# Other slots for the gate terms, the loads, the fold and the finishing of an mLSTM and Fourier-mix kernel

## The chip, the cores and the metric

The kernel runs on one core of a Trainium2 chip. Its time is the device time of one execution in microseconds (us). Several runs were taken, and the median of them stands for the kernel. One further execution was recorded by the hardware profiler. The engines are called PE or TensorE (matrix products; PEld is its weight load), DVE or VectorE, ACT or ScalarE, POOL or GpSimd, and SP or SyncE, which issues the DMAs here. Every engine works through its own instructions in the order of the program.

## The reference

Two blocks follow each other. The first is an mLSTM cell over batch 4, 8 heads, 768 steps and head size 40; the second is a Fourier mix with an MLP over rows of 8 * 40 = 320 features.

```python
for t in range(S):
    m_new = np.maximum(f_gate[:, :, t] + m, i_gate[:, :, t])
    f_stab, i_stab = np.exp(f_gate[:, :, t] + m - m_new), np.exp(i_gate[:, :, t] - m_new)
    C = f_stab[..., None, None] * C + i_stab[..., None, None] * np.einsum('bhd,bhe->bhde', vt, kt)
    n = f_stab[..., None] * n + i_stab[..., None] * kt
    h_tilde = np.einsum('bhde,bhe->bhd', C, qt)
    y[:, :, t] = sigmoid(o_gate[:, :, t]) * h_tilde / np.maximum(np.abs(n . qt), 1.0)
x = y as (B, S, 320)
u = x + real(fft(fft(x, axis=1), axis=2))
un = (u - mean(u)) / sqrt(var(u) + 1e-06)
out = u + np.maximum(un @ w_ch1, 0.0) @ w_ch2        # 320 -> 1280 -> 320
```

## The kernel before

All arithmetic is fp32. The recurrence is done in six chunks of 128 steps for each batch. A chunk needs the stabilising maximum, the decay and the weights of its steps; these gate terms are computed for all 32 (batch, head) rows at once in `gates`. Batch 0 works with whole chunks (`plan_mlstm`), batches 1 to 3 with half chunks (`plan_halves`), for which `gates_of_halves` makes other gate terms in nine numbered steps: step 0 the maxima at the half boundaries (GpSimd, with one VectorE instruction `nexts`, L327), step 1 the rows `keep` in the order of the chunks (ScalarE copies L335 to L341, GpSimd L342 and L343), step 2 one exponential of `between` (L345), twelve exponentials for the decays (L349), and all stores of `keep` and of the decays to the DRAM tensors `M_d` (12 DMAs, L357) and `G_d` (L359), step 3 twelve exponentials for the weights (L364), step 4 a GpSimd product (L368), steps 5 to 8 transposes and copies. The chunks of batches 1 to 3 read `M_d` and `G_d` back, spread over partitions, as `W` (L496) and `Gb` (L505).

A chunk of half-chunk kind goes through: loads (`mlstm_load`, `mlstm_load_max`, `mlstm_load_decay`), `qg` on GpSimd (`mlstm_scale_q`, L528), `vw` on GpSimd (`mlstm_scale_v`, L534), eight exponentials on ScalarE (`mlstm_exp`, L518), two masks on GpSimd (L543), scores and state sums on TensorE (`halves_scores`, `halves_to_state`, one PSUM tile of two banks), decay of the state on GpSimd (L696), add and weigh on VectorE (L703, L708), products with the state and the chunk on TensorE (`halves_from_state`, `halves_from_chunk`, a second PSUM tile), and `mlstm_finish` on VectorE (L752 to L759), which writes the rows of x.

The Fourier mix folds pairs of chunks (`mix_fold`, three pairs, VectorE and GpSimd), multiplies the folds with a table along the sequence (`mix_seq`, `mix_tail`, PSUM tiles `pz` and `pzt`), then along the features (`mix_feat`, `pu`), adds to x (`mix_add`), centres on ScalarE (`mix_center`), transposes on TensorE (`mix_turn`, `put`) and copies to `uT`. Before the change, batches 2 and 3 fold a second time (`mix_fold_again`, two VectorE instructions) and use the products of `mix_products_again`; batches 0 and 1 use `mix_products`. The MLP of batch 0 is plain (`mlp_in` L1067 and L1058, `mlp_relu`, `mlp_out` L1192); the MLPs of batches 1 to 3 go by blocks with fewer products (`mlp_block` L1129, `mlp_out_pair` L1248, `residual` L1198, `hidden_sums` L1234).

The weights come as float64 bits in ten pieces. Each is loaded, and rebuilt in fp32 by `take` (VectorE L436, L438), `convert` (ScalarE L443, L444) and `join` (VectorE L450, L452, L456).

The order of the work is written out by hand. `at(slot, phase, fn, ...)` puts a step into a slot and a phase in it, and `run` emits all in sorted order:

```python
def run(end=None):
    for key in sorted(plan):
        if end is None or key[0] < end:
            for fn, args in plan.pop(key):
                fn(*args)

EVAC, FILL, MAIN, FILL_PE = range(4)
```

So EVAC comes first in a slot, then FILL, MAIN and FILL_PE. Batch 0's mLSTM fills slots 0 to 21, its mix slots 18 to 28, its MLP slots 31 to 62 (`mlp_in` 31 to 50, `mlp_out` 51 to 62); the MLP of batch b begins at slot 31 + 32 b. Batch 1's mLSTM begins at slot 32 and its mix at 54; batch 2's at 51 and 83; batch 3's at 83 and 115. The step of chunk c counts from s = start + 3 c: scores at s, add and weigh at s + 1, from_state at s + 3, finish at s + 4. Two sets of memory change hands between two calls of `run`: the pool of the gates and four PSUM banks of batch 0 are closed, and the buffers of the later MLPs and the two PSUM tiles of the half chunks are opened; before, this is after slot 27.

PSUM tiles named by `bank` take one of four banks, either from a list written by hand (`turn`) or by a number. `idle_products` are products of zeros.

Of the kernel before, what the change touches and what calls it, by code (L numbers as in the profile page):

```python
# [19 lines left out]
L = 128  # L20
NT = S // L
NP = H // 2
# [35 lines left out]
def kernel(  # L58
# [83 lines left out]
    def idle_products(n, first=False):  # L142
        pw = bank("pi", [L, 2 * L]) if first else ps_s.tile([L, 2 * L], FP, name="pi", tag="ps")
        for i in range(n):
            nc.tensor.matmul(pw, rest[:, 0:L], rest, start=True, stop=True, skip_group_check=True)


    def gates(gp):
# [168 lines left out]
        def gates_of_halves(step):  # L317
# [15 lines left out]
            elif step == 1:  # L333
# [8 lines left out]
                nc.gpsimd.tensor_copy(out=W[:, 0:4:3, L - 1:L], in_=late["nexts"][:, 1:5:3])  # L342
                nc.gpsimd.tensor_copy(out=W[:, 4, LH:LH + 1], in_=late["nexts"][:, 5])  # L343
            elif step == 2:
                nc.scalar.activation(out=late["between"], in_=late["between"], func=AF.Exp)  # L345
                for c in range(NT):
                    for i in range(2):
                        t = slice(i * LH, (i + 1) * LH)
                        nc.scalar.activation(out=G[:, c, t], in_=W[:, c, t], func=AF.Exp, scale=-1.0,  # L349
                                             bias=late["starts"][:, c, i:i + 1])  # L350
                nc.sync.dma_start(out=sp_sb, in_=first_heads)
                for b in range(1, B):
                    for hip in range(2):
                        rows = slice(b * H + hip * NP, b * H + (hip + 1) * NP)
                        for i in range(2):
                            slot = slice(b * H + i * NP, b * H + (i + 1) * NP)
                            nc.sync.dma_start(out=M_d[:, i ^ hip, slot].rearrange("c p t -> p c t"),  # L357
                                              in_=W[rows, :, i * LH:(i + 1) * LH])
                nc.sync.dma_start(out=G_d[:, H:].rearrange("c p t -> p c t"), in_=G[H:BH])  # L359
            elif step == 3:  # L360
# [10 lines left out]
            elif step in (5, 7):  # L371
# [10 lines left out]
                if step == 5:  # L382
                    nc.tensor.matmul(late["pd"], spread_sb[:, 0:L], late["dec2"], start=True, stop=True)
            else:
                j = (step - 6) // 2
# [18 lines left out]
        at(7, FILL + 0.5, clear, fe[:, :, NC:PAD], fe[:, :, PAD + HALF_D - 1:], fe_odd[:, NC:])  # L404
        for n, (s, phase) in enumerate(((15, FILL + 0.75), (16, FILL + 0.75), (18, FILL + 0.75), (19, FILL + 0.75),
                                        (18, FILL + 0.8), (19, FILL_PE + 0.5), (20, FILL + 0.75),
                                        (21, FILL_PE + 0.5), (22, FILL + 0.75))):
            at(s, phase, gates_of_halves, n)
# [373 lines left out]
    def plan_halves(b, s0, stride=3):  # L782
        at(s0 - 2, FILL + 0.7, halves_start, b)
        for c in range(NT):
            s = s0 + stride * c
            end = c == NT - 1
            t = 22 + 2 * c if b == 1 and c < 3 else s - 6
            at(t, FILL, mlstm_load, b, c)
            at(t, FILL, mlstm_load_max, b, c)
            at(t + 1 if c < 2 or b > 1 else s - 5, FILL, mlstm_load_decay, b, c)  # L790
            at(s - 2, FILL, mlstm_load_o, b, c)
            at(s - 2, FILL + 0.1, mlstm_scale_q, b, c)
            at(s - 2, FILL + 0.15, halves_alone, b, c)
# [70 lines left out]
    def mix_seq(b, p, parts):  # L864
# [3 lines left out]
        if p == TG - 1:  # L868
            k.pz = getattr(k, "pz", []) + [bank("pz", [L, NK], MIX["z"][i] if b > 1 else None) for i in parts]
        for i in parts:  # L870
            if b < 2:
                mix_products(p, k.pz[i], i, slice(0, L))
# [4 lines left out]
    def mix_tail(b, p):  # L877

        k = mixes[b]
        if p == TG - 1:  # L880
            k.pzt = bank("pzt", [L, NK], MIX["zt"] if b > 1 else None)
        halves = [k.pzt[i * 64:(i + 1) * 64] for i in range(2)]
        if b < 2:
            for i in range(2):
# [43 lines left out]
    def mix_feat(b, p):  # L928
# [5 lines left out]
        m = slice(COL[p], COL[p] + L)  # L934
        pu = k.pu[p] = bank("pu", [L, DM + 1 + NC], MIX["u"][p] if b > 1 else None)
        if b == 0:
# [47 lines left out]
    def mix_turn(b, c):  # L984

        k = mixes[b]
        pt = k.pt[c] = bank("put", [L, 3, L], MIX["ut"][ORDER.index(c)] if b > 1 else None)
        for ch in range(3):
# [335 lines left out]
    def plan_batch(b, s_mlstm, s_mix, s_mlp):  # L1324
# [192 lines left out]
```

## Time and profile before

| what | us |
|---|---|
| median of three runs | 407.24 |
| lowest and highest run | 404.89, 408.12 |
| the profiled execution, its own time | 404.67 |
| span of its profile | 402.9 |
| TensorE idle after 30 us, the sum of its gaps of more than 0.1 us | 10.0 |
| first L1067 (slot 31) | 59.53 |
| first L1192 (slot 51) | 117.68 |
| first L1129 (slot 63) | 171.22 |
| first L1248 (slot 83) | 209.77 |

The profile is read like this. A row of a timeline has start, length, engine, line and operation, output and inputs, shapes, count, and in brackets the idle time of the engine ahead of it with what ended it. A row of the waits has who waited for whom, the total, the number of times and the longest. An fp32 product shows as two records. A row of the windows has the window, its length, the busy time and count of PE, PEld, DVE, ACT and POOL, the granted TensorE clock as a share of full speed, the DMA share and GB/s. The mean granted clock of the execution is 0.991.

### The profile page before, as it was taken

How to read it: one execution, taken by the hardware profiler on the slowest of the kernel's cores; microseconds unless marked ns; L12 is line 12 of the kernel's file. 1: busy time of each engine (PE TensorE's matmuls, PEld its weight loads, DVE VectorE, ACT ScalarE, POOL GpSimd, SP SyncE). 2: the span in 40 equal slices, each digit the busy share in tenths (PEclk: the TensorE clock that was granted, in tenths of full speed). 3: DMA queues.
4: the chain of work that ended last, by engine and by line, in shares of the span. 5: the costliest groups of instructions: out<-in, count | busy, mean ns of one | idle time of the engine just before them, and what ended most of it. 6: DMA issues, size and time to landing. Idle time of an engine off the chain costs nothing.

```text
span 402.9 us, 10837 instructions
## 1 busy us (share of the span) xinstructions
PE 387.8 (96%) x4324; PEld 283.3 (70%) x4324; DVE 279.8 (69%) x668; ACT 178.5 (44%) x513; POOL 128.0 (32%) x231
## 2 busy tenths in 40 slices
PE   8999999999969999999999998999999999999996
PEld 6887555556546776856569887855579997556996
DVE  7789976898867519787665689777663795336652
ACT  6898867576530213553562214544440023454000
POOL 5744425466945412261145304351200000020000
PEclk9999999989989999999999999999999999999999
DMA  7979499677752424365100525300000000000000
GB/s 197 278 227 320 121 240 257 194 242 240 191 151 70 142 87 131 109 196 150 54 26 2 157 82 170 103 20 2 1 0 18 17 34 33 2 0 0 34 34 34
DMA packets 22766, 43.96 MB, mean 109 GB/s; under 512 B 3492, under 2 KB 11388, under 8 KB 22588
## 3 DMA queue, kind: packets, MB, share of 16 engines
q1 hardware_dynamic: 22716, 43.27, 36.0%
q8 instruction: 34, 0.56, 0.5%
q14 instruction: 16, 0.13, 0.1%
HBM read 39.16 MB, written 4.10 MB: 107 GB/s over the span
## 4 chain that ended last, share of the span: by engine, by line
PE 80%; DVE 13%; issue 2%; POOL 2%; ACT 2%; DMA 0%; DVEq 0%; SPq 0%; POOLq 0%; ACTq 0%
PE po L1248 20%; PE pm L1129 16%; PE po L1192 8%; PE pm L1134 6%; PE ph L547 5%; PE ps L547 4%; PE pu L946 4%; PE pm L1067 4%; PE put L989 2%; PE pz L903 1%; PE pz L915 1%; DVE so L756 1%; PE pM L230 1%; PE pm L1058 1%; DVE x L759 1%
## 5 line engine op out<-in xcount | busy, mean ns | idle before, releaser
L1138 DVE TENSOR_TENSOR h<-h,pm 128x384 f32<-128x384 f32 x60 | 30.7, 550 | 30.6 <-PE pm L1129 16.5
L1198 DVE SCALAR_TENSOR_TENSOR x<-po,rstd,x 128x160 f32<-128x160 f32 (+1 forms) x69 | 27.0, 394 | 35.0 <-PE po L1248 32.3
L1129 PE MATMUL pm<-uT,w_sb 128*128 128x384 f32 x90 | 37.8, 507 | 0.2 <-DVE uT L1117 0.2
L543 POOL TENSOR_SCALAR_AFFINE_SELECT W<-W 64x512 f32<-64x512 f32 x36 | 27.9, 775 | 31.5 <-ACT W L518 30.4
L696 POOL TENSOR_TENSOR C<-C,decB 128x164 f32<-128x164 f32 x33 | 17.4, 528 | 62.1 <-DVE C L703 58.4
L518 ACT ACTIVATE W<-W,colT 128x64 f32<-128x64 f32 x144 | 36.5, 338 | 0.0
L1192 PE MATMUL po<-w_sb,h 128*128 128x320 f32 x120 | 35.2, 444 | 0.0
L1013 POOL TENSOR_TENSOR t<-rstd 128x6 f32<-128x6 f32 x12 | 2.6, 216 | 90.1 <-DVE v L1007 89.7
L1248 PE MATMUL po<-T,S 128*128 128x160 f32 x180 | 28.1, 303 | 2.6 <-DVE x L1198 2.6
L528 POOL TENSOR_TENSOR qg<-qk,Gb 128x512 f32<-128x512 f32 x21 | 27.3, 1298 | 9.5 <-DMA Gb<-G_d 9.5
L1192 PEld LDWEIGHTS po<-w_sb,h 128*128 128x128 f32 x120 | 22.7, 194 | 10.0 <-issue 1.5
L1067 PE MATMUL pm<-uT,w_sb 128*128 128x384 f32 x80 | 29.5, 505 | 0.1
L1248 PEld LDWEIGHTS po<-T,S 128*128 128x128 f32 x180 | 25.3, 190 | 4.5 <-DVE x L1198 3.4
L1248 PE MATMUL po<-w_sb,h 128*128 128x160 f32 x180 | 26.3, 300 | 0.0
L1248 PEld LDWEIGHTS po<-w_sb,h 128*128 128x128 f32 x180 | 25.2, 190 | 1.5 <-DVE x L1198 0.3
L994 ACT COPY uT<-put 128x384 f32<-128x384 f32 x24 | 11.1, 478 | 32.7 <-PE put L989 32.6
L1134 PE MATMUL pm<-uT,w1t_sb 64*128 64x384 f32 x120 | 25.2, 510 | 0.2 <-DVE h L1138 0.2
L1129 PEld LDWEIGHTS pm<-uT,w_sb 128*128 128x128 f32 x90 | 15.4, 189 | 14.0 <-DVE h L1138 4.9
L1185 ACT ACTIVATE h<-h 128x384 f32<-128x384 f32 x45 | 23.1, 520 | 2.0 <-DVE h L1138 2.0
L982 ACT ACTIVATE uc<-x 128x384 f32<-128x384 f32 x24 | 14.5, 614 | 18.9 <-DVE x L974 18.9
L703 DVE TENSOR_TENSOR C<-C,ps 128x164 f32<-128x164 f32 x33 | 10.5, 317 | 16.2 <-PE ps L547 13.6
L1067 PEld LDWEIGHTS pm<-uT,w_sb 128*128 128x128 f32 x80 | 14.5, 194 | 9.7 <-issue 1.4
(240 smaller groups left out, 860.8 us busy)
## 6 DMA issues: line engine op xcount, KB each, us to landing
kvt<-in_kv SPq DMA_DIRECT2D x24, 336.0 KB
qk<-in_qkT SPq DMA_DIRECT2D x48, 160.0 KB
raw<-in_w SPq DMA_DIRECT2D x10, 640.0 KB
Gb<-G_d SPq DMA_DIRECT2D x42, 128.0 KB
W<-M_d SPq DMA_DIRECT2D x36, 128.0 KB
so<-in_o SPq DMA_DIRECT2D x24, 160.0 KB
out<-x SPq DMA_DIRECT2D x24, 160.0 KB
ds_sb<-in_dft_s SPq DMA_DIRECT2D x1, 1158.0 KB
```

Of the source, the lines that this page charges most:

```text
L518: nc.scalar.activation(out=k.W[:, h, :], in_=M, func=AF.Exp, scale=-1.0, bias=colT[:, c, 0, b * H + h:b * H + h + 1])
L528: nc.gpsimd.tensor_tensor(out=k.qg[:, :, t], in0=k.qk[:, 0, :, t], in1=k.Gb[:, :, t], op=OP.mult)
L543: nc.gpsimd.affine_select(out=W, in_=W, compare_op=OP.is_ge, fill=0.0, base=base, pattern=[[0, H], [-1 if back else 1, LH]], channel_multi ...
L547: nc.tensor.matmul(out, w, x, start=start, stop=True, skip_group_check=True)
L1067: nc.tensor.matmul(k.pm[i], w1_sb[:, ch, f0:f0 + L], u[2 * ch], start=(ch == 0 and not ahead), stop=(ch == 1 and ahead), skip_group_check= ...
L1129: nc.tensor.matmul(bank, w, u, start=start, stop=True, skip_group_check=True)
L1134: nc.tensor.matmul(bank, block(w1t_sb, i)[rows], mlp_u(gr, 1)[rows], start=False, stop=True, skip_group_check=True)
L1138: nc.vector.tensor_tensor(out=h, in0=h, in1=bank, op=OP.add)
L1185: nc.scalar.activation(out=h, in_=h, func=AF.Relu, scale=-1.0)
L1192: nc.tensor.matmul(k.po, hidden(gr, f)[:, i * L:(i + 1) * L], w2_sb[:, f, :], start=(f == 0), stop=(f == NFF - 1))
L1198: nc.vector.scalar_tensor_tensor(out=u, in0=po, scalar=k.rstd[:, c:c + 1], in1=u, op0=OP.mult, op1=OP.add)
L1248: nc.tensor.matmul(po, a[:, f], w[:, f], start=start and f == 0, stop=f == half - 1, skip_group_check=True)
```

## The change

The gate terms of the half chunks are made earlier: step 0 in slot 8 for 15, step 1 in slot 10 for 16 and with the exponential of `between`, step 4 in slot 11 for 18. The stores leave step 2 and become steps of their own: `M_d` in slot 13, `G_d` in slot 20; steps 2, 3 and 5 to 8 stay. Batch 1's mLSTM begins at slot 29 for 32 and its mix at 51 for 54; its first three chunks are loaded in slots 15, 18 and 21 for 22, 24 and 26, with the decays in 21, 22 and 27. Its first scores and state sums go to slot 25 (vw to 24), and the change of memory is after slot 24. Batch 1 uses the second fold and its products, and the banks by number; `mlp_out` of batch 0 alternates banks 0 and 1. The last five weight pieces move by one slot at most and are taken and converted in one slot. `mlstm_finish` of batches 2 and 3 moves from FILL to behind MAIN of its slot. One idle product of three goes.

```diff
     def idle_products(n, first=False):
-        pw = bank("pi", [L, 2 * L]) if first else ps_s.tile([L, 2 * L], FP, name="pi", tag="ps")
+        if first:
+            pw = bank("pi", [L, 2 * L])
+        elif "heads" in banks:
+            pw = banks["heads"][:, 0, 0:2 * L]
+        else:
+            pw = ps_s.tile([L, 2 * L], FP, name="pi", tag="ps")
...
+                nc.scalar.activation(out=late["between"], in_=late["between"], func=AF.Exp)
             elif step == 2:
-                nc.scalar.activation(out=late["between"], in_=late["between"], func=AF.Exp)
...
-                nc.sync.dma_start(out=sp_sb, in_=first_heads)
-                for b in range(1, B):
...
-                nc.sync.dma_start(out=G_d[:, H:].rearrange("c p t -> p c t"), in_=G[H:BH])
...
+            elif step == 9:
+                nc.sync.dma_start(out=sp_sb, in_=first_heads)
+                for b in range(1, B):
...
+            elif step == 10:
+                nc.sync.dma_start(out=G_d[:, H:].rearrange("c p t -> p c t"), in_=G[H:BH])
...
-        for n, (s, phase) in enumerate(((15, FILL + 0.75), (16, FILL + 0.75), (18, FILL + 0.75), (19, FILL + 0.75),
-                                        (18, FILL + 0.8), (19, FILL_PE + 0.5), (20, FILL + 0.75),
-                                        (21, FILL_PE + 0.5), (22, FILL + 0.75))):
+        for n, (s, phase) in enumerate(((8, FILL + 0.75), (10, FILL + 0.75), (18, FILL + 0.75), (19, FILL + 0.75),
+                                        (11, FILL + 0.8), (19, FILL_PE + 0.5), (20, FILL + 0.75),
+                                        (21, FILL_PE + 0.5), (22, FILL + 0.75), (13, FILL + 0.9), (20, FILL + 0.9))):
...
-            t = 22 + 2 * c if b == 1 and c < 3 else s - 6
-            at(t, FILL, mlstm_load, b, c)
-            at(t, FILL, mlstm_load_max, b, c)
-            at(t + 1 if c < 2 or b > 1 else s - 5, FILL, mlstm_load_decay, b, c)
+            t, g = ((15, 21), (18, 22), (21, 27))[c] if b == 1 and c < 3 else (s - 6, s - 5)
+            at(t, FILL + 0.9, mlstm_load, b, c)
+            at(t, FILL + 0.9, mlstm_load_max, b, c)
+            at(g, FILL + 0.9, mlstm_load_decay, b, c)
...
-            at(s - 1, FILL, mlstm_scale_v, b, c)
+            first = b == 1 and c == 0
+            at(24 if first else s - 1, FILL, mlstm_scale_v, b, c)
...
-            at(s, FILL_PE + 2.05, halves_scores, b, c)
-            at(s, FILL_PE + 2.5, halves_to_state, b, c)
+            at(25 if first else s, FILL_PE + (5.6 if first else 2.05), halves_scores, b, c)
+            at(25 if first else s, FILL_PE + (5.6 if first else 2.5), halves_to_state, b, c)
...
-            at(s + 4 + int((b, c) in ((2, 2), (3, 1))), FILL + 0.05, mlstm_finish, b, c)
+            late = int((b, c) in ((2, 2), (3, 1)))
+            at(s + 4 + late, (FILL + 0.05 if b == 1 else MAIN + 0.4), mlstm_finish, b, c)
...
-            if b < 2:
+            if b == 0:
                 mix_products(p, k.pz[i], i, slice(0, L))
...
-            elif b == 1 or j == 0:
-                if b > 1:
-                    for step, slot in enumerate((x_done[-1] + 2, x_done[-1] + 6)):
-                        at(slot, FILL_PE + 0.25, mix_fold_again, b, step)
+            elif j == 0:
+                for step in range(2):
+                    at(*((x_done[-1], FILL + 0.55) if b == 1 else (x_done[-1] + 2 + 4 * step, FILL_PE + 0.25)),
+                       mix_fold_again, b, step)
...
-            k.po = bank("po", [L, DM])
+            k.po = bank("po", [L, DM], (gr * TG + i) % 2)
...
-            feat = [s_mix + c for c in ((3, 4, 6) if b == 1 else (3, 4, 7))]
-            add = [s_mix + c for c in ((4, 4, 5, 6, 7, 7) if b == 1 else (4, 4, 5, 6, 8, 9))]
-            turn = [s_mix + c for c in ((5, 6, 6) if b == 1 else (6, 7, 8))]
-            late = [s_mix + c for c in ((7, 8, 8) if b == 1 else (9, 10, 10))]
+            feat = [s_mix + c for c in (3, 4, 7)]
+            add = [s_mix + c for c in (4, 4, 5, 6, 8, 9)]
+            turn = [s_mix + c for c in (6, 7, 8)]
+            late = [s_mix + c for c in (9, 10, 10)]
...
-    plan_batch(1, 32, 54, s_mlp + MLP_SLOTS)
+    plan_batch(1, 29, 51, s_mlp + MLP_SLOTS)
...
-    when += [((33, 0.7), (35, 0.7), (36, 0.6))] + [((s, 0.7), (s + 1, 0.7), (s + 2, 0.6)) for s in (36, 39, 42, 45)]
+    when += [((s, 0.6), (s, 0.7), (s + 1, 0.6)) for s in (34, 37, 40, 43, 46)]
...
-    for s, phase, n in ((24, 5.5, 1), (25, 5.5, 1), (26, 5.5, 1)):
+    for s, phase, n in ((24, 5.5, 1), (26, 5.5, 1)):
         at(s, FILL_PE + phase, idle_products, n)
-    run(28)
+    run(25)
```

Where `if b > 1 else None` chose a bank of the mix before, it now reads `if b > 0 else None`, for `pz`, `pzt`, `pu` and `put`.

More of the change, by code (lines that the diff above doesn't have):

```diff
@@ L350, in gates_of_halves @@
                                              bias=late["starts"][:, c, i:i + 1])
-                nc.sync.dma_start(out=sp_sb, in_=first_heads)
-                for b in range(1, B):
[L353 to L358, printed above, removed]
-                nc.sync.dma_start(out=G_d[:, H:].rearrange("c p t -> p c t"), in_=G[H:BH])
             elif step == 3:
@@ L383, in gates_of_halves @@
                     nc.tensor.matmul(late["pd"], spread_sb[:, 0:L], late["dec2"], start=True, stop=True)
+            elif step == 9:
+                nc.sync.dma_start(out=sp_sb, in_=first_heads)
+                for b in range(1, B):
+                    for hip in range(2):
+                        rows = slice(b * H + hip * NP, b * H + (hip + 1) * NP)
+                        for i in range(2):
+                            slot = slice(b * H + i * NP, b * H + (i + 1) * NP)
+                            nc.sync.dma_start(out=M_d[:, i ^ hip, slot].rearrange("c p t -> p c t"),
+                                              in_=W[rows, :, i * LH:(i + 1) * LH])
+            elif step == 10:
+                nc.sync.dma_start(out=G_d[:, H:].rearrange("c p t -> p c t"), in_=G[H:BH])
             else:
@@ L868, in mix_seq @@
         if p == TG - 1:
-            k.pz = getattr(k, "pz", []) + [bank("pz", [L, NK], MIX["z"][i] if b > 1 else None) for i in parts]
+            k.pz = getattr(k, "pz", []) + [bank("pz", [L, NK], MIX["z"][i] if b > 0 else None) for i in parts]
         for i in parts:
-            if b < 2:
+            if b == 0:
                 mix_products(p, k.pz[i], i, slice(0, L))
@@ L880, in mix_tail @@
         if p == TG - 1:
-            k.pzt = bank("pzt", [L, NK], MIX["zt"] if b > 1 else None)
+            k.pzt = bank("pzt", [L, NK], MIX["zt"] if b > 0 else None)
         halves = [k.pzt[i * 64:(i + 1) * 64] for i in range(2)]
-        if b < 2:
+        if b == 0:
             for i in range(2):
@@ L934, in mix_feat @@
         m = slice(COL[p], COL[p] + L)
-        pu = k.pu[p] = bank("pu", [L, DM + 1 + NC], MIX["u"][p] if b > 1 else None)
+        pu = k.pu[p] = bank("pu", [L, DM + 1 + NC], MIX["u"][p] if b > 0 else None)
         if b == 0:
@@ L986, in mix_turn @@
         k = mixes[b]
-        pt = k.pt[c] = bank("put", [L, 3, L], MIX["ut"][ORDER.index(c)] if b > 1 else None)
+        pt = k.pt[c] = bank("put", [L, 3, L], MIX["ut"][ORDER.index(c)] if b > 0 else None)
         for ch in range(3):
```

## The prediction

> **What bounds the kernel now.** I read the busy table first, then a table of stages, then TensorE's waits, and then, inside the stages that lose time, the engines' timelines.
>
> ```profile
> PE 387.8 (96%) x4324; PEld 283.3 (70%) x4324; DVE 279.8 (69%) x668; ACT 178.5 (44%) x513; POOL 128.0 (32%) x231
> ```
>
> TensorE (PE) is the bound over the span of 402.9 us, so only TensorE time saved, or a TensorE wait removed, can pay. The stage table (window, length, busy PE, PEld, DVE, ACT, POOL, clock, DMA share, GB/s) says where there is any:
>
> ```profile
> 32.00:40.00 8.00, 7.10 (x106) 5.76 (x103) 7.51 (x22) 6.57 (x20) 3.46 (x10) 1.00 1.03 342
> 40.00:48.00 8.00, 7.15 (x53) 4.77 (x53) 7.21 (x19) 6.28 (x25) 4.90 (x10) 1.00 0.30 100
> 60.00:118.00 58.00, 53.91 (x920) 33.28 (x919) 46.41 (x98) 36.16 (x109) 35.31 (x53) 0.95 0.76 218
> 118.00:174.00 56.00, 56.00 (x750) 39.79 (x752) 36.20 (x92) 16.50 (x54) 21.50 (x30) 0.99 0.34 109
> ```
>
> 60 to 118 is batch 0's first MLP product with batch 1's mLSTM filled in (slots 31 to 50): 4.1 us idle, and the clock is below 1. From 118 on TensorE never stops. The waits of TensorE name the releasers:
>
> ```profile
> PE ph L547 <- DVE x L759: 3.1, 1, 3.1
> PE po L1248 <- DVE x L1198: 2.6, 2, 1.9
> PE ps L547 <- DVE C L703: 1.0, 1, 1.0
> PE ph L581 <- POOL qg L528: 0.9, 1, 0.9
> ```
>
> All the large ones are VectorE (DVE) being late. Two finer windows carry the half clock that follows:
>
> ```profile
> 80.00:88.00 8.00, 7.00 (x134) 5.14 (x126) 7.76 (x16) 5.75 (x17) 4.45 (x7) 0.79 0.72 228
> ...
> 112.00:120.00 8.00, 5.94 (x76) 3.68 (x77) 5.20 (x16) 3.29 (x12) 4.51 (x12) 0.79 0.48 138
> ```
>
> 0.79 over 8 us is 3.4 us at half rate, so 1.7 us lost each time, after the 1.0 and the 3.1 us wait. VectorE's own rows before the second:
>
> ```profile
> 109.77 1.77 DVE L456 TENSOR_TENSOR w_sb<-m,e 128x640 f32<-128x640 f32 x1
> 111.47 0.31 DVE L703 TENSOR_TENSOR C<-C,ps 128x164 f32<-128x164 f32 x1
> ...
> 113.52 0.49 DVE L759 TENSOR_TENSOR x<-ph,so 128x320 f32<-128x320 f32 x1
> ```
>
> A weight pass (L456, alone 0.82 us) stands ahead of the mLSTM work and takes 1.77, because GpSimd (POOL) runs a 1.84 us qg from 109.01. This recurs all over the trace: a VectorE row with all inputs in SBUF (L456, L756, L836) that starts during a GpSimd row ends one own length after it.
>
> **The change part by part.** The profiled execution is 404.67 us (span 402.9 and 1.77 around it); the median shown is 407.24. I work out differences and put them on the median.
>
> *(1) Gate terms, slots 15/16/18 to 8/10/11.* In the trace they stand here on GpSimd:
>
> ```profile
> 34.37 0.20 POOL L326 TENSOR_TENSOR a<-a,F 32x5 f32<-32x5 f32 x1
> ...
> 34.69 0.26 POOL L331 TENSOR_SCALAR less<-M 32x6 f32<-32x6 f32 x1
> 37.67 0.22 POOL L331 TENSOR_SCALAR less<-nexts 32x5 f32<-32x5 f32 x1 [2.73 <-DVE nexts L327]
> ...
> 38.47 1.25 POOL L528 TENSOR_TENSOR qg<-qk,Gb 128x512 f32<-128x512 f32 x1
> ```
>
> The queue stood 2.7 us for one small VectorE row, and chunk 5's qg behind it cost TensorE 0.9. In slot 8 the same knot recurs: nexts now follows the weight join of slot 8 (L450 25.25 to L456's end), so GpSimd waits from 24.95 to about 27.8 and then runs less, less, between (0.7), vw (0.73) and chunk 3's qg (1.24): qg ends at 30.5, where TensorE wants it at 29.14 (L581). That is a new wait of 1.3. It passes down TensorE's queue; ScalarE gets 1.2 us of copies and the exponential (L335 to L345) ahead of chunk 4's eight exponentials, so chunk 5's weights come 1.2 later (39.15 for 37.94). VectorE is contiguous from 25.25 to 49.15 and sets the end. It wins L456's stall (1.0) and, with L368 (0.84) gone from slot 18, most of L836's at 44.44 (0.9); it loses about as much where L756, L436 and L438 meet the crowded GpSimd at 29 to 37, and then waits for the exponentials. I get +1.0. Bounds: -2.0 (only the wins) and +3.9 (the whole 2.9 wait and one 1.0 stall). The DMAs: 12 M_d stores took 4.5 us of SP's queue at 41.0; now they stand at 31 to 36, ahead of chunk 5's so load (36.03, read at 43.28) and batch 1's first loads: 2 us late with 5 us of cover, zero. The G_d store stays behind its exponentials at slot 20; Gb of batch 1 still lands 2 us or more before slot 27's qg: zero; without that cover it costs what is left of the 1.27 us qg.
>
> *(2) Chunk (1,0)'s scores and state sums in slot 25* (two TensorE groups, 1.07 us at 63.15), where an idle product stood. TensorE is waiting there for ScalarE's centred rows (put at 57.20 and 58.41): 57.6 + 1.07 = 58.67, so the last put is 0.26 late: +0.3 (0 to +1.07). vw in slot 24 (0.74) has its data at 51.2. The dropped idle product (0.4) was inside the wait: 0.
>
> *(3) Slots 31 to 51, batch 1 three slots earlier, weight passes after the mLSTM's add.* Before: 59.53 to 122.55, the end of batch 2's first scores, 63.0 us. TensorE's work in it after the change: 80 records of L1067 by 0.355 start to start 28.4; 40 of L1058 by 0.2125 8.5; three put 1.0; one pu 1.8; mLSTM groups 3 by 1.88 (71.93 to 73.81), 2 by 2.33 (105.80 to 108.13), the last 1.08: 11.4; first half of po 2.7; batch 2's scores 1.07. Sum 54.9. Check on before: 54.9 + 1.07 + 4.1 idle + 3.4 lost to clock = 63.5 against 63.0. Waits that I expect in their place: 1.2 in slot 32 (chunk (1,0)'s eight exponentials can start only after the last uT copy, 59.47; 2.0 of them, 1.6 of masks, decay, add, so the state is ready at 63.9 where TensorE asks at 63.1, and the scores 0.4 later); 1.0 in slot 47 (from_state of chunk 5 needs finish of chunk 4; VectorE's period there is add and weigh 1.1, finish 1.65, weight pass 3.3, fold 1.9, stalls 0.9, so 8.9 against TensorE's 7); 1.6 in slot 49 (the relu that frees its bank stands on ScalarE behind the last piece's conversion, which waits for that late VectorE). 54.9 + 3.8 = 58.7: -4.3. Bounds: -8.1 (no wait) and -0.6 (waits and clock as before, the sum's 0.5 error off).
>
> A gap's after-cost is the clock. Here 1.0 and 3.1 us of wait were each followed by 3.4 us at half rate, while 1.85 us at 248.0 was followed by none; I put none on the shorter waits, 1.7 each in the bound. The Trainium skill, TensorE: Matmul & The Clock Gate (HAM oscillation), says instead that gaps hurt from about 3.4 us; by it neither dip of this trace would exist, the part would be worth 3.4 less wherever I count recovered clock, and 401.3 below would read 404.7. The rows decide.
>
> *(4) Folding batch 1 twice.* Batch 1's pz and pzt now: 132.63 to 134.72, 137.41 to 139.35, 142.14 to 144.28, 6.17 us. The same three pieces of batch 2, which already folds twice: 1.47 + 1.33 + 1.52 = 4.32. TensorE is full there: -1.85 (0 if VectorE's two added passes, 0.55 + 0.68, come last; -1.85 else). New banks and the two po banks: TensorE has no gap in 118 to 174 and each bank has two slots to drain: 0, or 0.35 per residual if not.
>
> *(5) Finishing of batches 2 and 3 behind the slot's products.* In slot 91 VectorE runs finish (247.80 to 249.44) before the residual that TensorE waits for, the 1.85 row; swapped, the residual is ready at 248.2: -1.65. In slot 87 finish began during the product; it now starts after the second residual (231.4) and ends at 233.0 for 232.44, which delays the next residual: +0.55. The other ten lie where TensorE did not wait: 0. Sum -1.1 (-1.65 to +0.55).
>
> Total: 1.0 + 0.3 - 4.3 - 1.85 - 1.1 = -5.95. **401.3 us** on the median (398.7 for the profiled run).
>
> **Rivals.** *B, all waits go.* If VectorE keeps up, (3) gives 3.8 more and (1), (2) nothing: 401.3 - 3.8 - 1.3 = 396.2. For it: VectorE is 80% busy in 60 to 118. Against: the last three periods, worked out above.
> *C, VectorE becomes the bound before slot 51.* Finish of chunk 5 (1.65), the last fold (1.9) and folding again (1.25) now come before batch 1's first pz; if none fits in, 4.8 of it shows: 406.1. For it: 46.4 of 58 us busy with the stalls in. Against: po and scores (3.8) cover it.
> *D, slower: the GpSimd knot of slot 8.* Price at most 2.9 (wait) + 2.7 (moved rows, in line ahead of qg) + 3.3 (VectorE shut out from 31.4 to 34.7 while GpSimd runs back to back) + 3.4 (two dips) = 12.3. Parts 3 to 5 pay 7.25, so from 7.25 it is slower than before; at 12.3 it is 412.3. Against: at 41 and 44 us VectorE waited out two rows, not five.
>
> **How the numbers follow.** The first forecast 0.48 (own range 398.5 to 404), B 0.18, C 0.20, D 0.14. About 1%, or 4.1 us, is what a measurement of this kernel can tell from none. Below 403.2: 0.42 of the first, all of B, 0.05 of C: 0.65. Above 411.3: half of D, 0.07. Rest 0.28. The range 395.5 to 409 leaves out a lower tail of B and the upper half of D.
>
> **What would show it.** (1) qg of chunk 3 ending near 30.5 with a TensorE wait on it, and the first L1067 near 60.8. (3) L1192 starting near 115 instead of 117.68, with no 3 us gap. (4) only L903 rows for batch 1, 4.3 us. (5) no 1.85 row on L1198. Wrong if the first L1067 comes before 59 or after 63, or if pz of batch 1 waits for folding.

## The result and the profile after

The changed kernel takes 406.79 us (median of 20 runs, 405.75 to 409.62), the kernel before 404.8 us in runs beside it: ratio 1.0064, 95% interval 1.004 to 1.0088. That is less than the 1% that the prediction calls no change, but the interval lies above 1: about 2 us slower, where 5.95 us faster were forecast. The forecast of 401.3 stood on the 407.24 of three runs; from 404.8 it would have been 398.9, so the miss is some 8 us, not the 5.5 between 406.79 and 401.3. The profiled execution has a span of 407.6 us for 402.9. Its own time, 409.38, is 2.6 above the median, so its stages show more loss than the medians do. Cut at the same events (most lines of the changed kernel are 5 to 9 higher: `mlp_in` L1067 is now L1076, `mlp_out` L1192 is L1201, L1129 is L1138, L1248 is L1257; the moved stores L357 and L359 are L387 and L390), the two spans, and those of two experiments told below, are:

| stretch, us | before | after | part 1 undone | and conversion later |
|---|---|---|---|---|
| start to first `mlp_in` | 59.53 | 64.43 | 58.96 | 59.26 |
| to first `mlp_out` | 58.16 | 62.30 | 58.25 | 54.92 |
| to the end of batch 2's first scores | 4.87 | 4.03 | 4.03 | 4.03 |
| to first `mlp_block` | 48.66 | 46.71 | 46.74 | 47.58 |
| to first `mlp_out_pair` | 38.55 | 38.33 | 38.33 | 38.33 |
| to the end | 193.17 | 191.76 | 191.73 | 191.76 |
| span | 402.94 | 407.56 | 398.06 | 395.88 |

All that was lost lies ahead of the first `mlp_out`, 9.0 us; behind it 4.4 us were won. The same windows of time as those shown of before; the first `mlp_in`, at 64.43, now falls inside the third:

```profile
32.00:40.00 8.00, 7.84 (x118) 6.53 (x115) 5.75 (x17) 6.19 (x19) 4.86 (x6) 1.00 0.99 362
40.00:48.00 8.00, 7.17 (x52) 4.51 (x50) 6.54 (x19) 2.41 (x8) 4.15 (x7) 1.00 0.38 102
60.00:118.00 58.00, 51.48 (x887) 31.66 (x885) 44.98 (x99) 32.12 (x94) 31.35 (x41) 0.94 0.78 217
118.00:174.00 56.00, 54.31 (x692) 38.77 (x689) 39.73 (x98) 19.60 (x60) 26.48 (x40) 1.00 0.35 105
```

In 60 to 118 TensorE is now idle 6.5 us for 4.1, and VectorE is no busier than before (44.98 for 46.41): VectorE waits too. TensorE's waits:

```profile
PE ph L554 <- DVE C L710: 3.4, 1, 3.4
PE ph L554 <- ACT warm L746: 2.9, 3, 1.7
PE p L377 <- ACT f_sb L360: 2.4, 6, 1.2
PE po L1257 <- DVE x L1207: 1.5, 2, 1.3
PE ph L588 <- POOL qg L535: 1.2, 1, 1.2
```

The fifth is the forecast's GpSimd knot in slot 8 (1.3 worked out, 1.18 measured), the fourth what is left of the finishing. The first and the third were not in the forecast. Both lead to SP, the queue of the DMA issues. SP's timeline before, the load of the o gate of chunk 5 (`so`), and then from the first store of `M_d` to the load of weight piece 4 (`raw`, L426):

```profile
36.03 0.33 SPq L511 DMA_DIRECT2D so<-in_o  x1
...
41.00 4.53 SPq L357 DMA_DIRECT2D M_d<-keep  x12
46.75 0.29 SPq L359 DMA_DIRECT2D G_d<-shift  x1
47.16 0.70 SPq L484 DMA_DIRECT2D qk<-in_qkT  x2
48.37 0.36 SPq L486 DMA_DIRECT2D kvt<-in_kv  x1
48.84 1.12 SPq L496 DMA_DIRECT2D W<-M_d  x2
50.05 1.19 SPq L505 DMA_DIRECT2D Gb<-G_d  x2
51.29 0.58 SPq L426 DMA_DIRECT2D raw<-in_w  x1
```

And after, from the loads of the two Fourier tables on:

```profile
32.05 1.62 SPq L475 DMA_DIRECT2D ds_sb<-in_dft_s  x1
33.72 0.42 SPq L476 DMA_DIRECT2D dd_sb<-in_dft_d  x1
...
34.72 9.04 SPq L387 DMA_DIRECT2D M_d<-keep  x12
43.86 0.36 SPq L518 DMA_DIRECT2D so<-in_o  x1
44.31 1.50 SPq L491 DMA_DIRECT2D qk<-in_qkT  x2
...
50.85 0.32 SPq L390 DMA_DIRECT2D G_d<-shift  x1
56.78 1.08 SPq L512 DMA_DIRECT2D Gb<-G_d  x2
...
61.82 0.53 SPq L433 DMA_DIRECT2D raw<-in_w  x1
```

SP's own waits in this stretch:

```profile
SPq L512 <- DMA G_d<-shift: 5.6, 1, 5.6
SPq L387 <- DMA ds_sb<-in_dft_s: 2.6, 1, 2.6
SPq L387 <- DMA dd_sb<-in_dft_d: 1.4, 1, 1.4
```

Two things went wrong in this one queue. The stores took 9.04 us for 4.53, and the o gate's load of chunk 5 behind them left at 43.86 for 36.03. A single store was issued about as fast as before (0.302 us in the median for 0.298); what was added is that SP stood still between two stores until the tables had landed, 2.6 and 1.4 us (DMA share 0.99 in 32 to 40). No store needs the tables: the trace has the sixth store wait for the transfer issued eight before it, which is the first table, and the seventh likewise for the second. ScalarE stood for the o gate's load, with all its exponentials behind, and TensorE waited for the transposes of these (L377):

```profile
46.54 0.47 ACT L641 ACTIVATE so<-so 128x320 f32<-128x320 f32 x1 [3.79 <-DMA so<-in_o]
46.91 2.96 ACT L354 ACTIVATE shift<-keep,starts 32x64 f32<-32x64 f32 x12
```

And the store of `G_d`, the fetch of `Gb` and the load of weight piece 4 now stand behind two or three chunks' loads. SP, at the fetch, waits 5.6 us for the store to land, with everything behind the fetch held up, though the DMA engines had little left to do (share 0.26 in 56 to 60; before 1.03). The piece leaves at 61.82 for 51.29, and VectorE, in order, waits 5.92 us for it with the mLSTM's add (L710) behind it, for which TensorE waits 3.38:

```profile
70.56 0.49 DVE L443 TENSOR_SCALAR e<-raw 128x640 uint32<-128x640 uint32 x1 [5.92 <-DMA raw<-in_w]
70.97 0.49 DVE L445 TENSOR_SCALAR m<-raw 128x640 uint32<-128x640 uint32 x1
71.37 0.32 DVE L710 TENSOR_TENSOR C<-C,ps 128x164 f32<-128x164 f32 x1
```

The clock of this execution was at half rate in 52.71 to 56.12 and 73.19 to 80.02, 5.1 us lost, behind these two waits.

### The profile page after: what moved, and what is told of

It is laid out like the page before. It is cut to its first block, busy times and chain, and to the rows that moved or that the text cites. A ratio compares the mean times of both kernels' runs of the same rounds, so it can differ in the third digit from the quotient of the medians.

```text
span 407.6 us, 10825 instructions
## 1 busy us (share of the span) xinstructions
PE 387.2 (95%) x4322; PEld 282.9 (69%) x4322; DVE 277.4 (68%) x670; ACT 178.3 (44%) x513; POOL 129.8 (32%) x231
## 4 chain that ended last, share of the span: by engine, by line
PE 79%; DVE 9%; ACT 5%; issue 3%; POOL 3%; DMA 1%; DVEq 0%; POOLq 0%; ACTq 0%
PE po L1257 20%; PE pm L1138 17%; PE po L1201 8%; PE pm L1143 6%; PE ph L554 5%; PE pm L1076 4%; PE pu L955 4%; PE ps L554 3%; PE pz L912 2%; PE put L998 2%; ACT W L525 1%; PE pzt L912 1%; PE pM L235 1%; DVE so L763 1%; POOL W L550 1%
## 5 line engine op out<-in xcount | busy, mean ns | idle before, releaser
L1147 DVE TENSOR_TENSOR h<-h,pm 128x384 f32<-128x384 f32 x60 | 30.5, 550 | 31.3 <-PE pm L1138 16.4
L1138 PE MATMUL pm<-uT,w_sb 128*128 128x384 f32 x90 | 37.7, 506 | 0.2 <-DVE uT L1126 0.2
L1201 PE MATMUL po<-w_sb,h 128*128 128x320 f32 x120 | 34.4, 435 | 0.0
L1076 PE MATMUL pm<-uT,w_sb 128*128 128x384 f32 x80 | 30.9, 526 | 0.1
L1257 PE MATMUL po<-T,S 128*128 128x160 f32 x180 | 28.1, 303 | 1.5 <-DVE x L1207 1.5
L1201 PEld LDWEIGHTS po<-w_sb,h 128*128 128x128 f32 x120 | 22.1, 190 | 9.3 <-issue 1.1
L1257 PEld LDWEIGHTS po<-T,S 128*128 128x128 f32 x180 | 25.3, 190 | 3.4 <-DVE x L1207 2.0
L1257 PE MATMUL po<-w_sb,h 128*128 128x160 f32 x180 | 26.3, 300 | 0.0
L1257 PEld LDWEIGHTS po<-w_sb,h 128*128 128x128 f32 x180 | 25.2, 190 | 1.5 <-DVE x L1207 0.3
L1138 PEld LDWEIGHTS pm<-uT,w_sb 128*128 128x128 f32 x90 | 15.6, 189 | 13.9 <-DVE h L1147 6.0
L1076 PEld LDWEIGHTS pm<-uT,w_sb 128*128 128x128 f32 x80 | 15.0, 200 | 10.0 <-issue 1.8
L541 POOL TENSOR_TENSOR vw<-kvt,colT 128x328 f32<-128x328 f32 x23 | 18.8, 818 | 9.2 <-ACT colT L398 7.4
```

The costliest lines, as they stand in the source:

```text
L1076: nc.tensor.matmul(k.pm[i], w1_sb[:, ch, f0:f0 + L], u[2 * ch], start=(ch == 0 and not ahead), stop=(ch == 1 and ahead), skip_group_check= ...
L1138: nc.tensor.matmul(bank, w, u, start=start, stop=True, skip_group_check=True)
L1147: nc.vector.tensor_tensor(out=h, in0=h, in1=bank, op=OP.add)
L1201: nc.tensor.matmul(k.po, hidden(gr, f)[:, i * L:(i + 1) * L], w2_sb[:, f, :], start=(f == 0), stop=(f == NFF - 1))
L1257: nc.tensor.matmul(po, a[:, f], w[:, f], start=start and f == 0, stop=f == half - 1, skip_group_check=True)
```

## The experiments

The expectations speak of these theories. Q: SP's queue, that is the order of stores and loads in slots 13 to 23. G: GpSimd's knot in slot 8. V: VectorE is the bound ahead of slot 51. After the first four runs, L: transfer order, with batch 1's early loads as its core; E: the early gate terms themselves. All ratios are to the kernel before on the same chip.

**The stores one slot later**, behind the o gate's load.

```diff
-                                        (21, FILL_PE + 0.5), (22, FILL + 0.75), (13, FILL + 0.9), (20, FILL + 0.9))):
+                                        (21, FILL_PE + 0.5), (22, FILL + 0.75), (14, FILL + 0.9), (20, FILL + 0.9))):
```

> The changed kernel with the sp_sb load and the 12 M_d stores one slot later (14 for 13), so that they stand behind the load of so for chunk (0,5) on SP's queue instead of ahead of it. Theory Q (SP's queue): the changed kernel lost 4.9 us before the first L1076 because that load was issued at 43.86 and landed at 46.5; with it issued near 35 ScalarE's exponentials are done by 50, TensorE's six waits on f_sb (2.4) and the half clock at 52.7 (1.7) go, the first L1076 comes at 60 to 61 instead of 64.4 and the time falls by about 4 us against the changed kernel. Theory G (GpSimd's knot in slot 8, with VectorE behind it): nothing of that changes, the first L1076 stays at 64. The late weight piece 4 stays as it is, so the wait near the start of the MLP should remain under both.

408.69 us in four runs, ratio 1.0100 (1.0039 to 1.0162). The wait for the exponentials is gone and the first `mlp_in` comes at 60.60 for 64.43, but the 4 us of theory Q do not come: the next wait grows from 3.4 to 7.1, and the first `mlp_out` comes at 126.19 for 126.73.

```profile
PE ph L554 <- DVE C L710: 7.1, 1, 7.1
```

VectorE waits 9.7 us for the same weight piece, for 5.9:

```profile
DVE e L443 <- DMA raw<-in_w: 9.7, 1, 9.7
```

The first delay had hidden a part of the second.

**Weight piece 4 ahead of the fetch of Gb(1,0).**

```diff
-            t, g = ((15, 21), (18, 22), (21, 27))[c] if b == 1 and c < 3 else (s - 6, s - 5)
+            t, g = ((15, 22), (18, 22), (21, 27))[c] if b == 1 and c < 3 else (s - 6, s - 5)
...
-             (14, mlstm_load_o, 5), (23, None, 4)]
+             (14, mlstm_load_o, 5), (22, None, 4)]
```

> The changed kernel with the load of weight piece 4 in slot 22 for 23, ahead of batch 1's first two decay loads, of which the first moves from slot 21 to 22. Theory Q: piece 4 is issued at 55 to 56 instead of 61.8, VectorE's 5.9 us wait for it goes, and with it the 3.4 us and 1.0 us waits of TensorE at 68 to 74 and the 3.4 us lost to half clock: 6 to 8 us faster than the changed kernel. Theory V (VectorE has too many passes before slot 51, the rival C of the prediction): VectorE's lateness at 110 to 122 stays and takes back most of what is gained, at most 3 us faster.

405.98 us, ratio 1.0040 (1.0004 to 1.0075). The wait for L710 falls from 3.4 to 0.8, the first `mlp_in` stays late (65.34). That is 0.8 us under the changed kernel, not the 6 to 8 of theory Q. **Both edits together:**

> Both of the last two edits together. Theory Q: first L1076 at 60 to 61, no wait over 1.5 us before 110 us, 10 to 12 us faster than the changed kernel, so 395 to 398 where the kernel before is at 404.8. Theory G: no better than the piece alone. Theory V: 401 or more.

406.32 us, ratio 1.0050 (1.0020 to 1.0079). The first `mlp_in` is on time (59.79), and TensorE waits again, 2.5 for GpSimd (L667) and 1.9 for L710, with 10.2 us at half rate: GpSimd's qg(1,0) now waits 12.3 us for `Gb`. In these three runs, whatever was put first in this stretch, the next was late, and theory Q in this form, one or two transfers put right, fails: its 395 to 398 don't come.

**Part 1 undone**, parts 2 to 5 kept: gate terms, stores and batch 1's first loads in the slots of before.

```diff
-        for n, (s, phase) in enumerate(((8, FILL + 0.75), (10, FILL + 0.75), (18, FILL + 0.75), (19, FILL + 0.75),
+        for n, (s, phase) in enumerate(((15, FILL + 0.75), (16, FILL + 0.75), (18, FILL + 0.75), (19, FILL + 0.75),
...
-                                        (21, FILL_PE + 0.5), (22, FILL + 0.75), (13, FILL + 0.9), (20, FILL + 0.9))):
+                                        (21, FILL_PE + 0.5), (22, FILL + 0.75), (18, FILL + 0.76), (18, FILL + 0.77))):
...
-            t, g = ((15, 21), (18, 22), (21, 27))[c] if b == 1 and c < 3 else (s - 6, s - 5)
+            t, g = ((22, 23), (24, 25), (26, 27))[c] if b == 1 and c < 3 else (s - 6, s - 5)
```

> The changed kernel with its first part undone: gate terms back in slots 15, 16 and 18, both stores in slot 18, batch 1's first loads back in slots 22 to 27; everything else as in the changed kernel. Theory Q: the queue is in the order of the kernel before (so of chunk 5 at 36, piece 4 near 51), so the losses go here too: 396 to 400, within 2 us of the run with both edits. Theory G: like Q here, since the knot of slot 8 is undone as well; the run with both edits then stays well above this one. Theory V: 402 or more.

399.79 us, ratio 0.9894 (0.9842 to 0.9947). So part 1 costs about 7 us and the rest pays about 4.5. Theory V falls: with all the folding and finishing in, TensorE's waits of 45 to 125 us are short (the 3.4 and the 2.4 are gone). That the run with both edits stays 6.5 us above this one is what G forecast; the next run parts G from the loads.

```profile
PE ph L554 <- ACT warm L746: 2.9, 3, 1.7
PE ps L554 <- POOL vw L541: 1.0, 1, 1.0
PE ph L554 <- DVE x L766: 0.6, 1, 0.6
```

**Gate terms early, loads late.** The first experiment's kernel with only the loads and decays moved back.

```diff
-            t, g = ((15, 21), (18, 22), (21, 27))[c] if b == 1 and c < 3 else (s - 6, s - 5)
+            t, g = ((22, 23), (24, 25), (26, 27))[c] if b == 1 and c < 3 else (s - 6, s - 5)
-            at(t, FILL + 0.9, mlstm_load, b, c)
+            at(t, FILL, mlstm_load, b, c)
...
```

> The changed kernel with its early gate terms kept (steps 0, 1 and 4 in slots 8, 10 and 11, the stores of M_d in slot 14, behind the load of the o gate of chunk (0,5)), but with the first three loads of batch 1 back in slots 22, 24 and 26 and their decays in 23, 25 and 27. Theory L: the whole cost of part 1 is transfer order, the bulk of batch 1's first loads in front of the store of G_d and of the fetches of Gb and of the weight pieces. Then the order is that of the run with part 1 undone, and this run takes 399 to 401 us, first mlp_in at 59 to 60 us, 58 to 59 us from there to the first po. Theory E: the early gate terms themselves cost (GpSimd's knot in slot 8, the wait of 1.18 us that it gives TensorE, exponentials in other slots): 403 us or more, and the time is lost ahead of 45 us. In between, 401 to 403, both have a share, and the landmarks say how much is ahead of the first mlp_in.

401.55 us, ratio 0.9914 (0.9885 to 0.9943): 7 us better than the first experiment. The early loads are the main cost. The early gate terms and stores are left with the 1.8 us to 399.79 (0.8 by the ratios, whose intervals overlap), and the first `mlp_in` is the later one, 61.44 for 58.96: theory E has at most this share, and theory G with it. The phase of these loads went from FILL + 0.9 to FILL too, for all batches, here, with part 1 undone and in the run with one early load. No run tries it alone. For the early loads themselves it can't change the order on SP: in the slots up to 21 no other issue stands between the two phases.

**The store of G_d ahead of the load of chunk (1,1)**, loads early, stores in slot 14, piece 4 first as above.

```diff
-                                        (21, FILL_PE + 0.5), (22, FILL + 0.75), (13, FILL + 0.9), (20, FILL + 0.9))):
+                                        (21, FILL_PE + 0.5), (22, FILL + 0.75), (14, FILL + 0.9), (18, FILL + 0.85))):
```

> The changed kernel with the stores of M_d in slot 14, the store of G_d moved ahead of the load of chunk (1,1) in slot 18, and weight piece 4's load in slot 22 ahead of the decay of chunk (1,0). Batch 1's first loads stay early. Theory L in its narrow form: what hurts is that the store of G_d stands behind these loads, so that Gb's fetch waits for its landing (5.6 us in the changed kernel) and GpSimd's qg(1,0) for Gb (12.3 us in the run with the stores and the piece both moved). With the store ahead, Gb's fetch waits under 1 us, the weight waits between 64 and 74 us are under 1 us in sum and the time is 400 to 402 us. Theory L in its wide form: the loads fill the queues in 48 to 60 us whatever the order, the raw weight piece lands as late as before: 404 us or more. Theory E (the early gate terms cost): 404 us or more too, but with the loss ahead of 45 us.

406.97 us, ratio 1.0041 (1.0011 to 1.007). The narrow form fails: the store left at 48.16, but the fetch of `Gb` follows the loads of (1,1), (1,2) and the piece (55.78), and GpSimd stands as long:

```profile
POOL qg L535 <- DMA Gb<-G_d: 12.4, 1, 12.4
```

**Only chunk (1,0) early.** The kernel with late loads, but this one load back in slot 15.

```diff
-            t, g = ((22, 23), (24, 25), (26, 27))[c] if b == 1 and c < 3 else (s - 6, s - 5)
+            t, g = ((15, 23), (24, 25), (26, 27))[c] if b == 1 and c < 3 else (s - 6, s - 5)
```

> The changed kernel with its early gate terms, the stores of M_d in slot 14, and of batch 1's early loads only that of chunk (1,0) (slot 15); those of chunks (1,1) and (1,2) back in slots 24 and 26, the decays in 23, 25 and 27. Theory L by bytes: the cost is in the bytes ahead of the fetches of Gb(1,0) and of weight piece 4 on SP's queue, which are then those of the run with all loads late: 400.5 to 402.5 us. Theory L by the slot: any early load that stands in front of the store of G_d and of the tables' transfers costs, about a third of the 7 us that the three cost: 403 to 405 us.

401.72 us, ratio 0.9927 (0.9899 to 0.9955), as with all late. So it isn't that a load stands in front, but how many: one chunk is ahead of the fetch of Gb(1,0) in both, three in the kernel above. Two were not tried. SP's timeline shows the piece leaving at 52.12, in front of chunk (1,1), though the fetch again waited 3.3 us for the store:

```profile
45.86 1.12 SPq L503 DMA_DIRECT2D W<-M_d  x2
47.09 0.48 SPq L390 DMA_DIRECT2D G_d<-shift  x1
50.95 1.08 SPq L512 DMA_DIRECT2D Gb<-G_d  x2
52.12 0.54 SPq L433 DMA_DIRECT2D raw<-in_w  x1
52.72 0.72 SPq L491 DMA_DIRECT2D qk<-in_qkT  x2
```

**The second fold alone**, in the kernel before, with its numbered banks and the alternating banks of `mlp_out`.

```diff
-            if b < 2:
+            if b == 0:
                 mix_products(p, k.pz[i], i, slice(0, L))
...
-            elif b == 1 or j == 0:
-                if b > 1:
-                    for step, slot in enumerate((x_done[-1] + 2, x_done[-1] + 6)):
-                        at(slot, FILL_PE + 0.25, mix_fold_again, b, step)
+            elif j == 0:
+                for step in range(2):
+                    at(*((x_done[-1], FILL + 0.55) if b == 1 else (x_done[-1] + 2 + 4 * step, FILL_PE + 0.25)),
+                       mix_fold_again, b, step)
```

> The kernel before with one part of the change alone: batch 1's rows folded a second time, as those of batches 2 and 3 were already, with the banks of its products numbered. The forecast's step (4) put this part at -1.85 us, all of it TensorE products left out between the first po and batch 2's first mlp_out. Alone, in slots that were not moved, it should give 402.2 to 403.2 us where the kernel before takes 404.5 (ratio 0.994 to 0.997). If the second fold needs the slots moved by three to be worth anything, or VectorE is too full there to take the fold's additions, the ratio is 0.998 or more.

406.42 us, ratio 1.0034 (0.9995 to 1.0073): no gain. The stretch to the first `mlp_block` is 48.68 us for 48.66, with two waits that the kernel before has not:

```profile
PE pm L1129 <- ACT uT L994: 0.9, 1, 0.9
PE put L989 <- ACT uT L994: 0.6, 1, 0.6
```

In the slots of before (feature products, adds and turns of batch 1 packed one or two slots tighter) the products left out uncover the chain from add over centring and turn to `uT`. In the changed kernel, with its looser slots, the same stretch has no such wait and is 1.95 shorter. That the looser list is the reason is argued, not tried alone.

**The finishing alone**, in the kernel before.

```diff
-            at(s + 4 + int((b, c) in ((2, 2), (3, 1))), FILL + 0.05, mlstm_finish, b, c)
+            at(s + 4 + int((b, c) in ((2, 2), (3, 1))), (FILL + 0.05 if b == 1 else MAIN + 0.4), mlstm_finish, b, c)
```

> The kernel before with one part of the change alone: the finishing products of batches 2 and 3 behind the main ones of their slot (MAIN + 0.4 for FILL + 0.05). The forecast's step (5) put this at -1.1 us; the gaps that it is meant for, at 236 and 248 us, were 0.75 and 1.85 us long, 1.29 and 0.21 us in the changed kernel. Alone it should give a ratio of 0.996 to 0.998. If the two waits only change places, or the half-rate windows that follow a wait decide, the ratio is 0.999 to 1.002.

402.86 us, ratio 0.9937 (0.9902 to 0.9972), the last stretch 191.76 for 193.17: 1.4 us by the profile. The waits of 0.75 and 1.85 became 1.29 and 0.21:

```profile
PE po L1248 <- DVE x L1198: 1.5, 2, 1.3
```

**The conversion of the last pieces.** Three tries on the kernel with part 1 undone, at its waits of 0.94 and 1.68 us for ScalarE's warm-up copy (L746, a copy of one element of the `ph` tile, after which the next products may start). First, VectorE's `take` of the pieces of slots 43 and 46 ahead of the folds (the expectation calls it convert; the phase that moves is that of the take):

```diff
-    when += [((s, 0.6), (s, 0.7), (s + 1, 0.6)) for s in (34, 37, 40, 43, 46)]
+    when += [((s, 0.6 if s < 43 else 0.45), (s, 0.7), (s + 1, 0.6)) for s in (34, 37, 40, 43, 46)]
```

> The changed kernel with part 1 undone (as in the run of that name, 399.79 us), and with the convert of the last two weight pieces (slots 43 and 46) put ahead of the folds' work in the order of its slot. There the first mlp_out waited 1.68 us and one earlier weight pass 0.94 us for ScalarE's warm-up convert, whose input stands behind these pieces' converts. If the order in the slot decides, both waits go and the time is 397 to 398.5 us. If ScalarE has no room in these slots at all, the waits stay and the time is 399.5 to 400.5 us; if the converts now hold up the folds' additions, the wait moves to the scores and the time is 400 us or more.

400.32 us, ratio 0.988 (0.9818 to 0.9941), nothing won on 399.79. The two waits went, and one of 2.3 took their place:

```profile
PE ph L554 <- DVE x L766: 2.3, 1, 2.3
```

Second and third, conversion and join two and three slots after the take, or one and two:

```diff
-    when += [((s, 0.6), (s, 0.7), (s + 1, 0.6)) for s in (34, 37, 40, 43, 46)]
+    when += [((s, 0.6), (s, 0.7), (s + 1, 0.6)) for s in (34, 37, 40)]
+    when += [((s, 0.6), (s + 2, 0.7), (s + 3, 0.6)) for s in (43, 46)]
```

> The changed kernel with part 1 undone (399.79 us in its run), and for the weight pieces of slots 43 and 46 ScalarE's conversion two slots later and VectorE's join three slots later than their take. ScalarE's warm-up copy, which TensorE waited for by 0.94 and 1.68 us, then no longer stands behind a conversion that waits for VectorE. If the order on ScalarE is the cause: both waits go, 2.6 us, and the time is 397 to 398 us. If VectorE is simply late there (it ran 46.4 of 58 us in the stretch before), the wait passes to its finishing rows and the time is 399.5 to 401 us, as when the take was put first.

> The same with the conversion one slot and the join two slots after the take, the spacing of the kernel before. Order on ScalarE as the cause: 397 to 398.5 us if one slot is enough to put the warm-up copies first, else one of the two waits stays and the time is 398.5 to 399.5 us. VectorE late: 399.5 to 401 us.

One slot later is 400.76 us, ratio 0.9917 (0.9882 to 0.9951), with a wait of 0.91 for the copy left, and one of 2.29, put down to GpSimd (L1025), in place of the other. Two slots later is **397.7 us, ratio 0.9835 (0.9797 to 0.9873)**, the best of all: both waits have gone, the stretch to the first `mlp_out` is 54.92 us for 58.25, and no half-rate window falls ahead of 395 us. The window of the other profile, at 67.06, is hardly what was won: here TensorE waits 1.4 us for ScalarE's centred rows in its place, and from the first `mlp_in` to the transposes (L998) that these rows feed the two profiles take 11.51 and 11.36 us.

```profile
PE put L998 <- ACT uc L991: 1.4, 1, 1.4
PE ps L554 <- POOL vw L541: 1.0, 1, 1.0
PE pz L912 <- DVE fe L871: 0.8, 1, 0.8
PE ph L554 <- DVE C L710: 0.3, 1, 0.3
PE ph L554 <- ACT warm L746: 0.3, 1, 0.3
```

ScalarE's order was the cause, since moving it by two slots alone removes both waits. That one slot was not enough because the take itself runs late is argued, from ScalarE's row with part 1 undone, where it idled 6.56 us for the take with the copy in line behind:

```profile
109.96 0.83 ACT L450 ACTIVATE e<-e,ebias 128x640 uint32<-128x640 uint32 x1 [6.56 <-DVE e L443]
```

## Why the prediction was wrong, point by point

*(1) Gate terms, +1.0 with bounds -2.0 and +3.9.* This is the step that failed. Undoing it wins 9.5 us of span (407.56 to 398.06), about 7 us of the medians. The knot on GpSimd was right in place and size: it waits 2.89 for `nexts`, as the 2.85 of the forecast, qg of chunk 3 ends at 29.6 (30.5 forecast), and TensorE waits 1.18 for it (1.3).

```profile
26.98 0.22 POOL L336 TENSOR_SCALAR less<-nexts 32x5 f32<-32x5 f32 x1 [2.89 <-DVE nexts L332]
...
28.34 1.26 POOL L535 TENSOR_TENSOR qg<-qk,Gb 128x512 f32<-128x512 f32 x1
```

Early gate terms with late loads, stores included, end at 401.55 for 399.79: 1.8 us, or 0.8 by the ratios, for the +1.0 of the sum. What failed is "The DMAs: ... 2 us late with 5 us of cover, zero" and "Gb of batch 1 still lands 2 us or more before slot 27's qg: zero". The stores were priced at 4.5 us, from a row in which SP waited little (0.6), and moved right behind the two tables, for whose landing it waited 4.0; they took 9.0, so the o gate's load left 7.8 late, not 2. And the moved loads of three chunks were put at nothing: they stand in the prediction as loads that the stores delay, not as work that `G_d`, `Gb` and the weight piece must queue behind. Moving them back is worth 7 us. Of the miss of some 8 us, this step is about 6 (7 for the 1.0 of the sum); the rest is that parts 2 to 5 pay 4.5 for the 6.95 forecast, chiefly in (3).

The Trainium skill, DMA: Bandwidth & Descriptors (Rules for kernel authors), says to overlap a DMA with compute by issuing it early and waiting for it late. No wait of TensorE in the kernel before was for batch 1's first loads; issuing three chunks of them early cost 7 us here (408.69 for 401.55), one chunk nothing that shows (401.72). The same table says that DMAs issued from several engines all run on the same 16 DMA engines. Here SP alone issued them, and in 32 to 40 they were busy by 0.99: early for one transfer was late for the next.

*(2) Scores in slot 25, +0.3.* With part 1 undone the first `mlp_in` comes at 58.96 for 59.53: no loss.

*(3) Slots 31 to 51, -4.3.* With part 1 undone the stretches to the end of batch 2's first scores take 62.28 us for 63.03: -0.75. The work was nearly right (62.28 less 5.03 of waits and 1.7 of clock is 55.5, for 54.9). The waits were 5.03 for 3.8, among them 1.68 for the copy behind the last conversion, which the forecast had at 1.6; and a window at half rate (67.06 to 70.48) was put at none. With the conversion two slots later the stretches take 58.95: -4.1, with 3.44 us of waits for 3.8. That this is so near is in part luck, for they are other waits: 1.37 for centred rows, 1.00 for vw, none for the conversion.

*(4) Second fold, -1.85.* -1.95 in its place (48.66 to 46.71), but alone nothing: the saving hangs on what stands around it, which the forecast left out.

*(5) Finishing, -1.1.* -1.4 in the changed kernel and alone. The two rows moved as worked out, +0.54 and -1.64 against +0.55 and -1.65; a third wait, 0.20 at 267.11, went with them. (That TensorE never stops from 118 on, as the prediction has it, holds to 174: these waits lie behind.)

*The rivals.* B's "all waits go" didn't happen; C's VectorE bound fell with 399.79. D had the right sign and the wrong place: a loss of some 7 us against gains of 4.5, but in the main through SP's queue and not GpSimd's.

## What to carry over

When a transfer is moved ahead, list what its queue then carries behind it, with bytes, and look in the trace at what that queue waits for in the stretch it moves into: a queue that stands for one landing holds up everything behind it. The price of an issue in the stretch that it leaves says nothing of this. A load that nothing waits for gains nothing by being early. When an engine runs behind its written slot, the engines it feeds must be given the order in which its results come, and a cut of one wait is worth only what the next in line leaves: try the parts alone.

## What the runs showed of the hardware

The time of a row of DMA issues is not that of the issues alone. The same 12 stores took 4.53 us before, 9.04 in the changed kernel and 8.63 with one early load; a single issue took 0.302 us in the median for 0.298, and most of the difference is SP waiting for landings between them (4.4 us in the changed kernel, 0.6 before). In every trace kept here, a DMA issue of SP that waited over 0.1 us for an earlier transfer waited for the one eight issues before it (13 times before, 11 in the changed kernel): its transfers signal on eight semaphores in turn. That comes from how this program issues; no run here has another number of them. For the landing of one small store (`G_d`, 72 KB), the fetch of `Gb` waited 3.3 us where the store was issued behind one chunk's loads and 5.6 us behind two; before, where it was issued ahead of them, there was no such wait.

Most of the spread of the kernel before goes with the granted clock: its executions at 0.996 spanned 400.1 to 402.4 us, those at 0.987 404.1 to 405.3. The half-rate stretches came as 3.41, 6.83 and 10.24 us. At one clock, 0.991, the kernel with the finishing alone spans 400.9 to 401.4 us in its four runs and the kernel before 402.2 to 405.1.

Such a stretch can stand behind waits of no more than 1 us, and longer ones can be followed by none. With part 1 undone, the last wait before the window at 67.06 was 1.00 us; with the conversion later, the same wait, 1.00 us, and another of 1.37 were followed by none. The Trainium skill, TensorE: Matmul & The Clock Gate (HAM oscillation), speaks of gaps over about 3.4 us; these rows don't agree with it as a lower bound, while the lengths are multiples of 3.41 us.
